# A reordered step list for chunked attention and a phase MLP: the first k pieces on ScalarE's queue, one tile in column halves

## The chip, the cores and the metric

The kernel runs on one core of a Trainium2 chip. The metric is the device time of one execution in microseconds (us). Engines are named as in the profile: PE is TensorE (PEld its weight loads), DVE is VectorE, ACT is ScalarE, POOL is GpSimd, SP is SyncE; a q behind a name (SPq, ACTq, POOLq) is the engine's sequencer that issues DMAs.

## The reference

q, k and v have the shape (8, 8, 576, 64): batch, heads, tokens, head size. Attention runs inside chunks of 64 tokens; its output, with the heads side by side, is the input x of a second block of width 512. All arrays are float32, and the computation cut to its core is:

```python
scores = 0.125 * np.matmul(q_c, k_c.transpose(0, 1, 2, 4, 3))   # per chunk of 64 tokens
attn = softmax(scores)
x = np.matmul(attn, v_c)                                        # (8, 576, 512) after reshaping
theta = x @ w_theta                                             # 512 x 512
zr, zi = x * np.cos(theta), x * np.sin(theta)
y = einsum('ts,bsd->btd', w_tok_r, zr) + einsum('ts,bsd->btd', w_tok_i, zi)   # 576 x 576 each
u = x + y
out = u + np.maximum(u @ w_ch, 0.0)                             # 512 x 512
```

## The kernel before, in words

**Tiles and groups.** Batches are handled in four pairs, p = 0 to 3. A batch has 576 tokens, 4 tiles of 128 and half a tile of 64. So a pair has nine tiles of 128 tokens: tiles 0 to 3 of its first batch, 4 to 7 of its second, and tile 8, which holds the last 64 tokens of both. Attention runs by groups: A (tiles 0 and 1), B (2 and 3), C (4 and 5), D (6 and 7) and M (tile 8). A step that works on a group is named by pair and group, "0A"; one that works on a tile by pair and tile, "31" is tile 1 of pair 3.

**The order.** Nothing is scheduled by a loop: ORDER is a list of some 560 steps, written out, and the kernel runs through it and emits each step's instructions. Every engine works through its own instructions in this order, and waits on semaphores for what others have to deliver. So ORDER decides, for each engine and each DMA queue, what stands behind what. A step has a kind, what it works on, and a number for the PSUM bank or the SBUF slot that it takes: "S.0B.6" are the scores of group B of pair 0 into bank 6.

**The kinds, by stage.**

- qk and v load a group's q and k, and v (two DMAs for q and k of a full group and four for M; three for v of a full group and two for M), with a cast to float16 on the way, from POOL's queue (L173, L178, L226). Group 0A alone is loaded in float32 by halves of its heads, qk0 and qk1, from SP's queue (L192), and cast by ACT and DVE (cy0, cy1; L210).
- T (or Tq and Tk apart; T0 and T1 for the halves of 0A) turns q and k on DVE by 32 x 32 blocks (L279). S are the scores on PE (L317), E their exponentials on ACT (L347, L359). V0 and V1 multiply with v on PE, four heads each (L381), N0 and N1 divide by the sums on DVE (L396, L398). The result is x.
- X turns x on PE (L413) and xa or xv copies it out of PSUM on ACT or DVE (L433, L431); xd does both in one transposing DMA from SP's queue (L425).
- H is theta on PE (L441; H0 and H1 for one tile each), G cosine and sine on ACT (L463, L464), Z the products zr and zi on DVE.
- lw loads a block of 128 rows of both token weights, lp theta's weights, lc the channel weights, all from POOL's queue (L236, L239, L242). TW turns a token block on PE (L257); twa and twv copy it out on ACT or DVE (L269, L267).
- Y is the token mixing of a tile on PE: nine products with the turned token weights (L521), for pair 0 in three parts, Ya, Yb and Ym. A adds x to it on DVE (L543); x then holds u.
- U turns u on PE (L548) and ua or uv copies it out; ud does both in a transposing DMA from SP's queue (L556). W is the channel product on PE, four products of 512 columns (L566). R is relu plus u on DVE (L571). st, sa and sg store the tile from SP's, ACT's or POOL's queue.
- dm issues matmuls on zeros that nobody reads.

Tile 37 has its channel product, its relu and its store in two column halves (W0, W1, R0, R1, sa0, sa1). The first steps of ORDER are, in words: both halves of 0A's q and k; both casts; T0.0A; then the loads of 0M, 0B, v of 0M, v of 0A, the second token block (lw.01), v of 0B, and theta's weights.

## Time and profile before

| what | value |
|---|---|
| median of 3 runs | 196.32 us (196.22 to 197.8) |
| profiled execution, its own time | 197.53 us |
| span of the profiled execution | 195.5 us |
| granted TensorE clock | 1.00 |
| busy PE / PEld / DVE / ACT / POOL | 176.8 / 91.2 / 136.4 / 84.6 / 89.4 us |
| DMA, moved | 31.99 MB, mean 164 GB/s |

The span runs from the first to the last event of the profiled execution; the profile's times count from its start, and 2.0 us of the execution's own time lie outside it. Busy times are sums over the span. Matmuls are pipelined, so a row of a matmul shows a duration of 380 ns where the next one starts 216 ns later; what a step of several matmuls takes is read from the chain of work, which merges a run of them. An entry in brackets behind a row is the idle time of that row's engine just ahead of it, and what ended it.

### The profile page before, as it was taken

How to read it: one execution, taken by the hardware profiler on the slowest of the kernel's cores; microseconds unless marked ns; L12 is line 12 of the kernel's file. 1: busy time of each engine (PE TensorE's matmuls, PEld its weight loads, DVE VectorE, ACT ScalarE, POOL GpSimd, SP SyncE). 2: the span in 40 equal slices, each digit the busy share in tenths (PEclk: the TensorE clock that was granted, in tenths of full speed). 3: DMA queues.
4: the chain of work that ended last, by engine and by line, in shares of the span. 5: the costliest groups of instructions: out<-in, count | busy, mean ns of one | idle time of the engine just before them, and what ended most of it. 6: DMA issues, size and time to landing. Idle time of an engine off the chain costs nothing.

```text
span 195.5 us, 5940 instructions
## 1 busy us (share of the span) xinstructions
PE 176.8 (90%) x2572; PEld 91.2 (47%) x2572; DVE 136.4 (70%) x245; ACT 84.6 (43%) x107; POOL 89.4 (46%) x128
## 2 busy tenths in 40 slices
PE   1159699969999899999999999999999999999975
PEld 0138355535554554645564434554443444454432
DVE  0446778777788796956986999598718845764742
ACT  4135099625955578497026295620096301200010
POOL 8999479895696479559997000000000100000310
DMA  5999999999999999999999968254668906989876
GB/s 161 179 174 174 189 170 167 121 164 172 127 107 170 169 110 167 179 166 160 125 146 171 125 126 213 46 207 121 134 80 191 269 17 121 235 221 280 286 190 215
DMA packets 103849, 31.99 MB, mean 164 GB/s; under 512 B 95248, under 2 KB 99728, under 8 KB 103824
## 3 DMA queue, kind: packets, MB, share of 16 engines
q0 software_dynamic: 76160, 17.59, 96.1%
q1 hardware_dynamic: 24912, 9.31, 21.5%
q10 hardware_dynamic: 2752, 4.72, 7.5%
q8 instruction: 20, 0.33, 0.7%
q14 instruction: 5, 0.04, 0.1%
HBM read 33.06 MB, written 9.44 MB: 217 GB/s over the span
## 4 chain that ended last, share of the span: by engine, by line
PE 77%; DMA 8%; POOL 4%; DVE 3%; SPq 2%; issue 2%; ACT 2%; POOLq 0%
PE psum L521 35%; PE psum L566 15%; PE psum L441 11%; PE psum L317 5%; PE psum L381 4%; DMA mid<-x 3%; PE psum L413 3%; DMA v<-in_v_dram 3%; DMA uT<-x 2%; SPq L556 2%; PE psum L257 1%; PE psum L548 1%; POOL v L226 1%; DVE x L398 1%; POOL big L173 1%
## 5 line engine op out<-in xcount | busy, mean ns | idle before, releaser
L521 PE MATMUL psum<-zr,wT 128*128 128x512 f16 (+1 forms) x180 | 62.2, 382 | 1.5 <-issue 1.5
L521 PE MATMUL psum<-zi,wT 128*128 128x512 f16 (+1 forms) x180 | 59.2, 380 | 0.0
L521 PEld LDWEIGHTS <-wT 128*128 128x128 f16 (+1 forms) x360 | 30.4, 100 | 35.3 <-issue 2.6
L226 POOL DMA_DIRECT2D v<-in_v_dram x56 | 41.9, 786 | 10.3 <-DMA big<-in_k_dram 5.0
L614 POOL DMA_DIRECT2D out_dram<-mid x6 | 3.3, 551 | 76.3 <-ACT big L463 45.9
L566 PE MATMUL psum<-wch,uT 128*128 128x512 f16 (+1 forms) x148 | 35.1, 374 | 1.0 <-DMA uT<-x 1.0
L441 PE MATMUL psum<-wtheta,mid 128*128 128x512 f16 x144 | 34.6, 388 | 0.8 <-DMA mid<-x 0.5
L543 DVE TENSOR_TENSOR x<-psum,x 128x512 f16<-128x512 f32 x36 | 24.1, 682 | 10.5 <-PE psum L521 10.5
L347 ACT ACTIVATE mid<-psum 128x1024 f16<-128x1024 f32 (+1 forms) x19 | 17.5, 932 | 31.5 <-PE psum L317 27.8
L571 DVE SCALAR_TENSOR_TENSOR mid<-psum,x 128x512 f32<-128x512 f32 (+1 forms) x37 | 24.3, 669 | 7.8 <-PE psum L566 6.4
L463 ACT ACTIVATE big<-psum,pihalf 128x1024 f16<-128x1024 f32 x14 | 15.6, 1113 | 29.3 <-PE psum L441 29.2
L398 DVE TENSOR_TENSOR x<-psum,recip 128x512 f16<-128x512 f32 (+1 forms) x40 | 25.5, 638 | 1.4
L279 DVE STREAM_TRANSPOSE big<-big 128x1024 f32<-128x1024 f32 (+3 forms) x25 | 24.5, 1007 | 0.3 <-DMA big<-in_k_dram 0.2
L441 PEld LDWEIGHTS <-mid 128*128 128x128 f16 x144 | 13.9, 100 | 17.8 <-DMA mid<-x 1.5
L566 PEld LDWEIGHTS <-uT 128*128 128x128 f16 x148 | 13.4, 98 | 15.9 <-DMA uT<-x 1.5
L317 PE MATMUL psum<-big 32*64 32x64 f16 x1152 | 14.8, 199 | 6.2 <-DVE big L279 6.2
L317 PEld LDWEIGHTS <-big 32*64 32x64 f16 x1152 | 12.8, 112 | 11.8 <-DVE big L279 8.1
L396 DVE RECIPROCAL recip<-psum 128x8 f32<-128x8 f32 (+1 forms) x40 | 7.8, 194 | 12.2 <-PE psum L381 12.2
L490 DVE TENSOR_TENSOR zr<-x,big 128x1024 f16<-128x1024 f16 x14 | 9.6, 686 | 9.0 <-ACT big L463 8.8
L151 ACT ACT_TABLE_LOAD x12 | 15.4, 1283 | 0.9 <-PEq L672 0.7
L560 ACT COPY uT<-psum 128x512 f16<-128x512 f16 x8 | 4.6, 590 | 24.0 <-PE psum L548 24.0
L178 POOL DMA_DIRECT2D big<-in_q_dram x15 | 13.8, 917 | 2.0 <-DMA big<-in_k_dram 1.0
(45 smaller groups left out, 150.2 us busy)
## 6 DMA issues: line engine op xcount, KB each, us to landing
out_dram<-mid ACTq DMA_DIRECT2D x16, 256.0 KB, 2.9
big<-in_q_dram POOLq DMA_DIRECT2D x15, 256.0 KB, 6.7
big<-in_k_dram POOLq DMA_DIRECT2D x15, 256.0 KB, 7.3
v<-in_v_dram POOLq DMA_DIRECT2D x40, 64.0 KB, 5.2
out_dram<-mid SPq DMA_DIRECT2D x9, 256.0 KB, 3.0
v<-in_v_dram POOLq DMA_DIRECT2D x16, 128.0 KB, 5.7
out_dram<-mid POOLq DMA_DIRECT2D x6, 256.0 KB, 3.2
out_dram<-mid SPq DMA_DIRECT2D x6, 128.0 KB, 2.8
```

The lines of the kernel that those rows point to most:

```text
L151: nc.scalar.activation(out=first, in_=pihalf, func=func)
L226: nc.gpsimd.dma_start(v16[rows, slot + t, :, 0:D], v[b, :, t0 : t0 + m, :].rearrange("h s d -> s h d"),)
L279: nc.vector.transpose(out.bitcast(FP32).rearrange("p (x l s) -> p x s l", l=32, s=2), in_.bitcast(FP32).rearrange("p (x s d) -> p x s d", ...
L317: nc.tensor.matmul(ps[half[r ^ cc], r, h], t[quarter[c], 1, h, :, e], t[quarter[c], 0, h, :, e], start=(e == 0), stop=(e == 1), tile_posit ...
L347: nc.scalar.activation(out=eT[:, 0:n].rearrange("p r h i -> p (r h i)"), in_=st.pop(("ps_s", p, g)).rearrange("p r h i -> p (r h i)"), fun ...
L398: nc.vector.tensor_tensor(out=x.rearrange("p r (h d) -> p r h d", h=HH), in0=ps[:, :, :, 0:D], in1=recip[:, 0:n].broadcast_to((P, n, HH, D ...
L441: nc.tensor.matmul(ps, xT[:, a, :], wtheta16[:, a, :], start=(a == 0), stop=(a == NDB - 1))
L463: nc.scalar.activation(out=cos, in_=ps, func=AF.Sin, bias=pihalf, scale=1.0)
L521: nc.tensor.matmul(ps[half[b]] if j == MID else ps, w, z, start=(kt == 0), stop=(kt == 2 * KT),)
L543: nc.vector.tensor_tensor(out=x, in0=st.pop(("ps_y", p, j)), in1=x, op=ALU.add)
L566: nc.tensor.matmul(ps, uT[:, a, :], wch16[:, a, cols], start=(a == 0), stop=(a == NDB - 1))
L571: nc.vector.scalar_tensor_tensor(out=out, in0=ps, scalar=0.0, in1=x, op0=ALU.max, op1=ALU.add)
```

## The change

ORDER is written anew from end to end, and three things are done in another way.

- The halves of 0A's k are issued by ACT's queue; those of q stay on SP's. The first half's casts are the other way round (cx0: q on DVE, k on ACT), and T0.0A comes ahead of the second half's casts.
- Behind M's q and k, POOL's queue now has v of 0A, q and k of 0B, v of 0B, theta's weights, v of 0M, and only then the token weights. Group D of pair 0 comes ahead of group C, from its loads to its theta.
- Tile 31 is worked on in column halves from the mixing on: Y0 and Y1 (nine products of 256 columns each), A0 and A1, U0 and U1 (two blocks each), uv0 and uv1 (copies on DVE), Wp (both halves of the channel product with the first two blocks), W0 and W1 (the other two), R0 and R1, st0 and st1. Tile 37 goes back to whole steps, and is the last one.

The numbers of turned and copied tiles by engine change little: X by PE 13 before and after, ud 26 before and 25 now, xa 5 and 8, xv 8 and 5, ua 8 and 6, uv 2 and 4 (and two halves), twa 3 and 1, twv 2 and 4. Of the 35 whole stores SP, ACT and POOL issued 12, 17 and 6 before (and ACT the two halves); now it is 8, 16 and 11 (and SP the two halves). dm goes from ten matmuls to nine.

What POOL issues first, before (big is the array of slots for q, k and the token weights; v_72 is v):

```order
L173 DMA big<-in_q_dram 32x8x128 x2
L173 DMA big<-in_k_dram 32x8x128 x2
L178 DMA big<-in_q_dram 128x8x128
L178 DMA big<-in_k_dram 128x8x128
L226 DMA v_72<-in_v_dram 64x8x64 x2
L226 DMA v_72<-in_v_dram 128x8x64
L226 DMA v_72<-in_v_dram 64x8x64 x2
L236 DMA big<-in_moe_w_tok_r_dram 128x576
L236 DMA big<-in_moe_w_tok_i_dram 128x576
L226 DMA v_72<-in_v_dram 128x8x64
L226 DMA v_72<-in_v_dram 64x8x64 x2
L239 DMA wtheta_69<-in_moe_w_theta_dram 128x4x512
```

and in the change:

```order
L174 DMA big<-in_q_dram 32x8x128 x2
L174 DMA big<-in_k_dram 32x8x128 x2
L227 DMA v_72<-in_v_dram 128x8x64
L227 DMA v_72<-in_v_dram 64x8x64 x2
L179 DMA big<-in_q_dram 128x8x128
L179 DMA big<-in_k_dram 128x8x128
L227 DMA v_72<-in_v_dram 128x8x64
L227 DMA v_72<-in_v_dram 64x8x64 x2
L240 DMA wtheta_69<-in_moe_w_theta_dram 128x4x512
L227 DMA v_72<-in_v_dram 64x8x64 x2
L179 DMA big<-in_q_dram 128x8x128
L179 DMA big<-in_k_dram 128x8x128
```

The three issues of v of 0A have moved ahead of q and k of 0B, theta's weights have moved from behind a token block to ahead of v of 0M, and the rows of the token weights are no longer among the first twelve; q and k of 0D stand there.

What DVE runs first, before (the casts of 0A's k, the turning, then the divisions of 0A):

```order
L146 MEMSET pihalf 128x1
L210 CAST big<-big 128x512 x2
L279 STREAM_TRANSPOSE big<-big 128x8x2x32
L279 STREAM_TRANSPOSE big<-big 64x8x2x32 x2
L279 STREAM_TRANSPOSE big<-big 128x8x2x32 x3
L396 RECIPROCAL recip<-psum 128x8
L398 TENSOR_TENSOR x<-psum,recip 128x2x256
L396 RECIPROCAL recip<-psum 128x8
L398 TENSOR_TENSOR x<-psum,recip 128x2x256
L431 COPY mid<-psum 128x1024
```

and in the change:

```order
L147 MEMSET pihalf 128x1
L211 CAST big<-big 128x512
L280 STREAM_TRANSPOSE big<-big 128x8x2x32
L280 STREAM_TRANSPOSE big<-big 64x8x2x32
L211 CAST big<-big 128x512
L280 STREAM_TRANSPOSE big<-big 128x8x2x32 x2
L397 RECIPROCAL recip<-psum 128x8
L399 TENSOR_TENSOR x<-psum,recip 128x2x256
L280 STREAM_TRANSPOSE big<-big 128x8x2x32
L280 STREAM_TRANSPOSE big<-big 64x8x2x32
L397 RECIPROCAL recip<-psum 128x8
L399 TENSOR_TENSOR x<-psum,recip 128x2x256
```

T0.0A and Tq.0M (64 rows) stand ahead of the second cast now; Tq.0B stands ahead of the first division of 0A, and Tk.0B and Tk.0M ahead of the second.

The end of SP's queue, before (stores and the transposes of ud):

```order
L614 DMA out_dram<-mid 128x512 x2
L556 DMA_TRANSPOSE uT<-x 128x4x128 x5
L614 DMA out_dram<-mid 128x512
L556 DMA_TRANSPOSE uT<-x 128x4x128
L614 DMA out_dram<-mid 128x512 x2
L556 DMA_TRANSPOSE uT<-x 128x4x128 x2
L614 DMA out_dram<-mid 128x512
L611 DMA out_dram<-mid 64x512 x2
L614 DMA out_dram<-mid 128x512
```

and in the change:

```order
L665 DMA out_dram<-mid 128x512 x2
L556 DMA_TRANSPOSE uT<-x 128x4x128 x8
L665 DMA out_dram<-mid 128x512
L556 DMA_TRANSPOSE uT<-x 128x4x128
L665 DMA out_dram<-mid 128x512
L672 DMA out_dram<-mid 128x256 x2
```

One store (st.25) is left between the last nine transposes, where three stood between the last eight; the last transpose is ud.37, and the last two stores are the halves of tile 31.

The code, and the first and last lines of ORDER, in the diff:

```diff
-qk0.0A.0 init.00 pre.00 qk1.0A.1 cy0.0A.2 cy1.0A T0.0A.0 on.00 qk.0M.3 qk.0B.4 v.0M dm.1.0
-S0.0A.2 E0.0A.0 Tq.0M.1 Tk.0M v.0A dm.1.0 T1.0A lw.01.3 v.0B S.0M.1 Tq.0B.5 Tk.0B lp.00 S1.0A.2
-E1.0A V1.0A.4 E.0M.1 V0.0A.0 V0.0M.2 lw.02.4 qk.0C.0 N1.0A S.0B.6 N0.0A E.0B.2 V1.0M.4 X.0A.5
-xv.0A.1 N1.0M TW.01.6 V1.0B.0 N1.0B V0.0B.3 N0.0B X.0B.5 twv.01 H0.0A.6 H1.0A.7 xv.0B.2 H1.0B.5
-lw.03.5 H0.0B.3 G0.0A.0 N0.0M X.0M.6 Z0.0A lw.00.1 G1.0A.1 qk.1M.3 qk.0D.2 G1.0B.0 TW.02.1 v.0C
-Tq.0C.6 Tk.0C xa.0M.2 H.0M.5 Z1.0A G0.0B.3 Z0.0B Z1.0B G.0M.1 TW.03.6 v.1M Z.0M twa.03 Ya.01.3
...
-R.36.2 R.30.6 sg.36 R.24.12 sg.25 Y.31.1 ud.32.6 sa0.37 st.17 A.27 st.30 ud.38.3 sa.22 W.38.2
-R.35.2 W.32.5 A.31 R.38.6 U.31.1 sa1.37 R.32.11 sg.33 ud.27.0 W.27.2 st.24 st.38 ua.31.5 W.31.1
-R.27.9 sa.27 dm.8.5 R.31.12 sg.35 sa.31 st.32
+qk0.0A.0 init.00 on.00 qk1.0A.1 pre.00 qk.0M.2 cx0.0A.3 T0.0A.4 v.0A Tq.0M.0 cy1.0A dm.1.0
+S0.0A.2 E0.0A.0 T1.0A S1.0A.0 qk.0B.5 v.0B lp.00 E1.0A V1.0A.2 V0.0A.0 v.0M Tq.0B.1 N1.0A Tk.0B
+Tk.0M S.0B.4 E.0B.1 V0.0B.2 qk.0D.4 lw.03.5 S.0M.4 E.0M.0 N0.0A N0.0B lw.01.1 V1.0B.5 N1.0B
+X.0A.0 xa.0A.1 v.0D X.0B.4 V0.0M.0 H1.0A.5 xv.0B.2 lw.02.0 V1.0M.4 N1.0M H0.0A.6 G1.0A.3 H1.0B.4
+G0.0A.0 N0.0M Tq.0D.2 Tk.0D G1.0B.1 H0.0B.0 G0.0B.2 X.0M.6 xv.0M.4 qk.0C.4 TW.03.2 twv.03
+qk.1M.5 Z1.0A H.0M.4 S.0D.2 G.0M.5 Z0.0A TW.01.0 v.0C lw.00.1 Z0.0B Ya.03.6 twv.01 Ya.01.4
+TW.02.0 Z1.0B v.1M Z.0M qk.1A.0 E.0D.3 twa.02 V1.0D.2 Yb.03 Ym.03 qk.1B.2 V0.0D.0 Ya.02.5
...
+W.21.4 R.21.8 ud.25.1 ud.30.5 R.20.10 sg.24 ud.38.6 W.38.7 R.38.0 R.33.5 Y.36.0 Y.37.7 sg.21
+U0.31.3 A.36 sg.20 W.25.0 A.37 R.25.10 sg.33 uv0.31.1 Y1.31.7 ud.35.4 A1.31 W.30.0 R.30.5
+ud.36.3 W.36.7 U1.31.3 sg.38 sa.17 sa.22 ud.34.6 sg.30 W.35.0 st.25 R.36.2 sg.36 ud.37.0
+Wp.31.7.2 uv1.31 W0.31 W1.31 W.34.3 R.35.10 W.37.0 R0.31.0 R1.31 R.34.5 sa.34 st.35 dm.8.2
+R.37.2 st1.31 st0.31 sa.37
...
-            for w, ap in enumerate((q, k)):
-                nc.sync.dma_start(
+            for w, (ap, queue) in enumerate(((q, nc.sync), (k, nc.scalar))):
+                queue.dma_start(
...
+    def mix_half(f):
+        def products(p, j, b):
+            st["ps_y", p, j, f] = banks(b)[:, 0 : DM // 2]
+            y_mms(p, j, KTS[""], st["ps_y", p, j, f], columns[f])
+
+        return products
...
+    def w_part(p, j, b0, b1):
+        for c, b in enumerate((b0, b1)):
+            st["ps_w", p, j, c] = banks(b)[:, 0 : DM // 2]
+            w_mms(p, j, c, blocks[0])
+
+    def w_mms(p, j, c, a_blocks):
+        for a in a_blocks:
+            nc.tensor.matmul(
+                st["ps_w", p, j, c], st["uT", p, j][:, a, :], wch16[:, a, columns[c]],
+                start=(a == 0), stop=(a == NDB - 1),
+            )
```

More of the change, by code (lines that the diff above doesn't have):

```diff
@@ L521, in y_mms @@
                 nc.tensor.matmul(
-                    ps[half[b]] if j == MID else ps, w, z,
+                    ps[half[b]] if j == MID else ps, w, z[:, cols],
                     start=(kt == 0), stop=(kt == 2 * KT),
@@ L562, in u_copy, with channel_mms @@
         return copy
[L564 removed]
+    def channel_mms(ps, uT):
         for a in range(NDB):
             nc.tensor.matmul(
[L567 removed]
+                ps, uT[:, a, :], wch16[:, a, :], start=(a == 0), stop=(a == NDB - 1)
             )
```

110 lines of the change are left out of this document (65 added, 45 removed).

## The prediction

> **What bounds the kernel now.** I read the windows first, cut at the places where TensorE starts a new stage. Columns: window and length, then busy time (and instructions) of PE, PEld, DVE, ACT and POOL, the granted clock, the DMA share and GB/s.
>
> ```profile
> 0.00:9.11 9.11, 0.61 (x2) 0.11 (x3) 1.79 (x5) 2.72 (x4) 8.50 (x18) 1.00 0.98 169
> 9.11:16.88 7.77, 5.31 (x209) 4.14 (x209) 4.72 (x9) 2.08 (x4) 7.39 (x11) 1.00 1.98 169
> 16.88:22.09 5.21, 3.62 (x58) 3.18 (x59) 3.57 (x8) 2.11 (x3) 3.08 (x6) 1.00 1.35 190
> 22.09:29.51 7.42, 7.13 (x47) 3.57 (x45) 4.87 (x12) 5.41 (x10) 5.15 (x8) 1.00 1.47 176
> ...
> 41.23:109.48 68.25, 66.22 (x1164) 35.42 (x1165) 54.28 (x98) 38.49 (x48) 50.92 (x68) 1.00 1.82 152
> 109.48:183.14 73.66, 73.12 (x761) 34.10 (x760) 52.78 (x91) 24.40 (x27) 2.21 (x5) 1.00 0.67 160
> 183.14:191.36 8.22, 7.21 (x37) 3.11 (x36) 4.22 (x7) 0.59 (x1) 1.08 (x3) 1.00 0.82 245
> ```
>
> From 22.09 to 191.36 PE is idle for only 3.9 us (0.29, 0, 2.03, 0.54 and 1.01): there the matrix work itself sets the time. Before 22.09 it is idle for 12.5 us (8.50, 2.46, 1.59). So a reordering can gain at the start, or lose anywhere. What ended PE's idle times later on is in the waits of PE (us, times, longest):
>
> ```profile
> PE psum L413 <- DVE x L398: 1.6, 1, 1.6
> PE psum L521 <- issue: 1.5, 1, 1.5
> PE psum L566 <- DMA uT<-x: 1.0, 1, 1.0
> ```
>
> A division on VectorE is late once, and a transpose by DMA near the end. The "issue" of 1.53 waits for nothing that the profile shows; with one more of 0.50 it makes the 2.03 of the fifth window. The timeline of the first 30 us has the two larger waits, for the turned q and k and for v, in brackets, and the steps behind them:
>
> ```profile
> 4.46 0.43 DVE L210 CAST big<-big 128x512 f16<-128x512 f32 x1 [3.59 <-DMA big<-in_k_dram]
> 5.02 0.90 POOL L178 DMA_DIRECT2D big<-in_q_dram  x1
> 5.91 0.90 POOL L178 DMA_DIRECT2D big<-in_k_dram  x1
> 6.78 3.65 POOL L226 DMA_DIRECT2D v<-in_v_dram  x5
> 7.80 0.63 DVE L210 CAST big<-big 128x512 f16<-128x512 f32 x1 [2.91 <-DMA big<-in_k_dram]
> 8.36 3.06 DVE L279 STREAM_TRANSPOSE big<-big 128x512 f32<-128x512 f32 x5
> 9.11 0.64 PE L317 MATMUL psum<-big 32*64 32x64 f16 x32 [6.24 <-DVE big L279]
> ...
> 11.65 0.71 DVE L279 STREAM_TRANSPOSE big<-big 128x512 f32<-128x512 f32 x1 [0.23 <-DMA big<-in_k_dram]
> ...
> 13.90 0.50 PE L381 MATMUL psum<-v,mid 64*64 64x65 f16 x3 [2.13 <-DMA v<-in_v_dram]
> 14.15 0.79 POOL L239 DMA_DIRECT2D wtheta<-in_moe_w_theta_dram  x1
> ...
> 16.48 1.02 ACT L347 ACTIVATE mid<-psum 128x1024 f16<-128x1024 f32 x1 [3.56 <-PE psum L317]
> ...
> 22.09 4.68 PE L441 MATMUL psum<-wtheta,mid 128*128 128x512 f16 x16
> ...
> 29.51 0.39 PE L521 MATMUL psum<-zr,wT 128*128 128x512 f16 x1
> ```
>
> At 8.36 T0.0A follows both casts, though its own half had landed by 4.46. PE's first scores come at 9.11, its first v product at 13.90, its first theta product at 22.09, its first mixing at 29.51. The chain of work that ended last gives v's landing and the prices of whole steps:
>
> ```profile
> 9.68 4.89 DMA v<-in_v_dram
> ...
> 28.95 0.62 PE psum L257 x10
> ...
> 32.35 0.64 PE psum L317 x64
> ...
> 55.40 0.25 PE psum L381 x16
> ...
> 175.41 0.88 PE psum L566 x8
> ...
> 183.14 4.49 DMA uT<-x
> ...
> 189.80 1.73 PE psum L566 x8
> ```
>
> So TW costs 0.62, a full S 0.64, half a V pair 0.25, four matmuls of 512 columns 1.73 / 2 = 0.86, eight of 256 columns 0.88.
>
> **The start, step by step.** (1) The halves. k leaves on ScalarE's queue, and T0.0A no longer stands behind the second half's cast: with k landed at 4.46 and 0.63 for a cast, as the second took, T0.0A starts near 5.1 and S0.0A near 5.8, 3.3 us earlier. That alone buys nothing, for PE then waits for T1.0A, which VectorE reaches only after Tq.0M (M's q, issued as before) and the second cast. I put T1.0A at 9.7, S1.0A near 10.2 and E1.0A at 10.9. The queue itself is costed at zero: what hides it is (2).
>
> (2) v of group A. Before, the third of its DMAs left at 9.68 and landed 4.89 later, at 14.57. Now the three follow M's four, from 5.02, at 3.65 / 5 = 0.73 apiece, so the last leaves at 6.5 and lands at 11.4. V1.0A moves from 13.90 to 11.4.
>
> (3) The price of that is group B's q and k, pushed back by three v issues, 2.2 us. k was issued at 5.91 and its turn began at 11.65, 5.74 later; now 8.1 + 5.74 = 13.85. This is what counts next: Tk.0B to 14.5, S.0B (0.64, and up to 1.07 as it ran in this stretch) to 15.4, E.0B 1.02 to 16.5, V0.0B, S.0M and V1.0B to 17.3, then N0.0B and N1.0B on VectorE. These are rows of VectorE by form:
>
> ```profile
> L398 DVE TENSOR_TENSOR x<-psum,recip 128x512 f16<-128x512 f32 x32 | 22.1, 691 | 1.1
> ...
> L396 DVE RECIPROCAL recip<-psum 128x8 f32<-128x8 f32 x32 | 6.4, 200 | 11.8 <-PE psum L381 11.8
> L279 DVE STREAM_TRANSPOSE big<-big 128x512 f32<-128x512 f32 x8 | 5.2, 678 | 0.2 <-DMA big<-in_k_dram 0.2
> ...
> L503 DVE TENSOR_TENSOR zr<-x,mid 128x512 f16<-128x512 f16 x4 | 1.7, 413 | 2.1 <-ACT mid L463 2.1
> ...
> L267 DVE COPY wT<-psum 128x1152 f16<-128x1152 f16 x2 | 1.5, 752 | 0.4 <-PE psum L257 0.4
> ```
>
> Two divisions of 0.89 from 16.9 end at 18.7, X.0B ends near 19.2, and H1.0A starts at 19.3 against 22.09: 2.8 us earlier. Its two inputs are there: theta's weights leave after v.0B, at 8.98 + 2.2 = 11.2 where it was 14.15, and xa.0A ends near 19.
>
> (4) From H1.0A to the first mixing. PE's own work is four H (3.44), V1.0M (0.13), X.0M (0.23), TW.03, H.0M, S.0D and TW.01: 6.5 us, to 25.8. VectorE is the longer one: two N of M, half a division each (1.2 with the short reciprocals), q and k of D (1.36), M's copy (0.4, as for one tile), twv.03 (0.75) and two Z of a tile (1.66) from 20.7, with a wait for X.0M, end at 26.6. So Ya.03 starts at 26.6 against 29.51, 2.9 earlier, with equal work behind it (S.0D for TW.02).
>
> (5) Behind it VectorE stays without a pause to about 35 (Z0.0B, twv.01, Z1.0B, Z.0M, N and T of D, C and the next M), and Ym.03 waits for Z.0M at 30.8. I take 0.4 off: **2.5 us of lead**. Bounds: 0.5 if every load here lands 2 us later than its median, 3.4 if the whole gain of v reaches the end and Tk.0B is not late.
>
> **The token weights.** They now leave behind v and theta. lw.03 leaves near 15.3 and TW.03 is wanted near 23.4. The DMA issues, with the median us to landing last, say:
>
> ```profile
> big<-in_moe_w_tok_r_dram POOLq DMA_DIRECT2D x4, 144.0 KB, 7.3
> ...
> uT<-x SPq DMA_TRANSPOSE x26, 3.2
> ```
>
> 16.0 + 7.3 = 23.3: in time with 0.1 to spare, so zero here; if they take as long as the slowest v (11.1, below), 3.7.
>
> **Tile 31 in halves.** Its mixing becomes 18 matmuls of 256 columns, its channel product 8; tile 37 goes back from 8 halves to 4 full ones. Eight halves took 0.88 against 0.86 for four full, so the columns cost 0.1 at most; the extra seams between steps cost 0.11 each (a step of four stands at 0.97 in the chain where another precedes it, at 0.86 in a run), some three of them, 0.3. The Trainium skill, TensorE: Matmul & The Clock Gate, section The mechanism, says that a weight load overlaps matmuls in flight only where its row group differs. These loads use all rows, so by that rule each half would pay for its load. The chain's 0.88 for eight halves disagrees: with loads of 98 ns ahead of each it would be 1.6.
>
> **The end.** The last product is now W.37, then R.37 and a 256 KB store, as W.31, R.31 and such a store are now. From the last matmul's end, 189.80 + 1.73 = 191.5, to the span's end stay 4.0 us. Before, W.38 waited 1.01 for a transpose that took 4.49 from issue to landing. Now ud.38 leaves 3.3 us ahead of W.38 and ud.37, behind st.25, about 4.0 ahead of W.37, counted back in PE work. The tiles' own rows:
>
> ```profile
> DMA to landing us min/median/max: 2.4/3.2/5.5
> ...
> DMA to landing us min/median/max: 3.2/5.5/11.1
> ```
>
> (the first for uT, the second for v). By the median nothing waits, by 4.49 1.2 plus 0.5, by the longest 2.2. I take 0.7, 0.3 less than now; with the seams the end is even.
>
> **The "issue" gaps**, 1.53 and 0.50, sit in stretches of many tiny matmuls. The new order keeps as many of these, so I leave the gaps in: zero, bounds -2.0 and +1.5.
>
> **Sum.** Lead 2.5, token weights 0, seams +0.3, transposes -0.3, gaps 0: the span goes from 195.5 to 193.0. The profiled execution took 197.53, 2.0 outside its span and 1.2 over the median; taken off the median, 196.32 - 2.5 = **193.8 us**, 1.3% less.
>
> **Rivals.** *The loads take the lead back.* For it: POOL is busy for 50.9 of the 68 us up to 109.48, the DMA share is above 1.3 in every window shown from 9.11 to there, and steps (3) and the token weights have less than half a microsecond to spare. Against it: the first 22 us leave out v.0M and a token block ahead of theta. With landings 2 us late the lead is 0.5: 195.8. Chance 0.22.
>
> *More than the lead.* If the gaps of 1.53 and 0.50 are an accident of where the program stood, they go: 193.8 - 2.0 = 191.8. For it: only two such gaps stand in the whole trace. Against it: nothing in the profile says what makes them, so nothing says that the new order is spared. Chance 0.15.
>
> *Slower: VectorE blocked in its order.* Tq.0B, Tk.0B and Tk.0M now stand ahead of the divisions of group A, and Tq.0M ahead of the second cast. If k of B takes longer to land than 5.74, all behind it moves one for one, and the lead is gone at 5.74 + 2.5 = 8.2. At the 11.1 of the slowest v the start is 2.9 worse than now: 199.2. Against it: with so little issued ahead, nothing has landed that late before 10 us. Chance 0.10.
>
> *The weight loads show.* If the loads of the halves were not hidden, nine more of 98 ns (nine for the mixing, four for the channel product, four fewer for tile 37) would add 0.9: 194.7. The row:
>
> ```profile
> L566 PEld LDWEIGHTS <-uT 128*128 128x128 f16 x148 | 13.4, 98 | 15.9 <-DMA uT<-x 1.5
> ```
>
> Chance 0.03, since the chain shows them hidden; this is what the Trainium skill's rule, above, would do here. That the halves on ScalarE's queue do not come earlier is no case of its own, since V1.0A waits for v either way.
>
> **How the numbers follow.** The forecast has 0.50, its own range 192.8 to 195.0. The 80% range runs from 191.9 (the second rival) to 196.4 (past the first); the slower rival stays outside. A measurement tells about 1% from no change: 194.36 and 198.28. Below lie two thirds of the forecast (0.34), the second rival (0.15) and a little of the others (0.04): faster 0.53. Above lies most of the slower rival: 0.09. The rest is 0.38.
>
> **What would show it.** Right: the first L317 near 6, V1.0A near 11.4, the first theta product near 19.3, the first L521 near 26.6, and from there the same idle as now. Wrong in (3): Tk.0B later than 14. Wrong for the token weights: PE waits at L257. Wrong at the end: PE waits for uT by more than 1. If the first L521 comes at 26.6 and the end does not move, the lead was lost to waits that PE had not had.

## The result and the profile after

The changed kernel takes **199.13 us** (median of 20 runs, 197.13 to 202.16); the kernel before, on the same chip, 197.35 (20 runs, 194.76 to 199.83). The ratio is 1.0121, 95% interval 1.0093 to 1.0149: 1.2% slower. (The ratio is taken over the runs within 1.5% of the fastest of their kernel, here and below; the two medians alone give 1.009.) The forecast was 193.8, 1.3% faster, with 0.09 on slower. (The three runs that it started from, 196.32, were on the low side of before's twenty.) The profiled execution of the change took 198.12 us with a span of 196.4 (before: 197.53 and 195.5), so the two profiled executions lie 0.6 us apart where the medians lie 1.8 apart. Line numbers shift: the scores are now L318, v L382, X L414, theta L442, TW L258, the dummies L163; the mixing stays L521, W L566, the relu L571.

The windows of TensorE's stages come first, cut at the first scores, the scores of group B, the first theta product and the first mixing, and from 41.23 on at the times of the windows of before (the columns are the same):

```profile
6.21:14.33 8.12, 1.94 (x98) 1.54 (x99) 3.97 (x8) 1.57 (x3) 8.12 (x11) 1.00 1.79 143
14.33:21.07 6.74, 5.36 (x152) 4.48 (x153) 3.54 (x8) 3.03 (x4) 4.00 (x7) 1.00 1.67 184
21.07:29.21 8.14, 8.14 (x120) 4.17 (x117) 5.26 (x14) 6.82 (x13) 5.90 (x10) 1.00 1.48 169
...
41.23:109.48 68.25, 67.06 (x1164) 35.02 (x1163) 55.34 (x97) 41.97 (x53) 51.47 (x68) 1.00 1.82 158
109.48:183.14 73.66, 72.86 (x769) 34.49 (x768) 49.55 (x89) 26.43 (x30) 5.45 (x10) 1.00 0.63 156
183.14:191.09 7.95, 7.36 (x47) 4.07 (x46) 5.45 (x11) 0.00 (x0) 1.64 (x4) 1.00 0.85 232
```

From the first theta product (21.07) to the first mixing (29.21) TensorE has no pause at all: 8.14 of 8.14 us. I had priced that stretch at 6.5 us of its work. The timeline of the start shows where the price fails:

```profile
6.21 0.64 PE L318 MATMUL psum<-big 32*64 32x64 f16 x32 [2.71 <-DVE big L280]
...
10.94 0.66 PE L382 MATMUL psum<-v,mid 64*64 64x65 f16 x32 [0.70 <-ACT mid L360]
...
14.32 1.07 PE L318 MATMUL psum<-big 32*64 32x64 f16 x64 [2.73 <-DVE big L280]
...
16.52 0.72 PE L382 MATMUL psum<-v,mid 64*64 64x65 f16 x16 [1.12 <-ACT mid L348]
17.17 1.06 PE L318 MATMUL psum<-big 32*64 32x64 f16 x32
18.16 0.44 PE L382 MATMUL psum<-v,mid 64*64 64x65 f16 x16
18.53 2.00 PE L414 MATMUL psum<-id,x 128*128 128x128 f16 x16
...
21.07 1.89 PE L442 MATMUL psum<-wtheta,mid 128*128 128x512 f16 x4
...
23.25 2.81 PE L442 MATMUL psum<-wtheta,mid 128*128 128x512 f16 x12
...
26.87 1.04 PE L442 MATMUL psum<-wtheta,mid 128*128 128x512 f16 x4
...
29.21 0.39 PE L521 MATMUL psum<-zr,wT 128*128 128x512 f16 x1
```

The first scores (6.21), the first v product (10.94) and the scores of group B (14.32) are where the forecast had them (near 6, 11.4, 14.5). Behind them the same four theta products take 1.89 us at 21.07 and 1.04 at 26.87: start to start they are (1.89 - 0.61) / 3 = 0.43 us apart at first and (1.04 - 0.39) / 3 = 0.22 later, with 0.61 and 0.39 the rows of a single product of that size, a dummy at 2.9 and the first mixing. TensorE runs at half its rate until about 23.4. The page's row PEclk shows 9 in every slice here, and the windows 1.00, so the products' spacing tells it and the granted clock of the page does not.

The waits of TensorE behind the start, by what ended them (total, times, longest):

```profile
PE psum L382 <- ACT mid L348: 1.1, 1, 1.1
PE psum L318 <- issue: 0.8, 1, 0.8
PE psum L566 <- ACT big L465: 0.8, 1, 0.8
...
PE psum L566 <- DMA uT<-x: 0.6, 1, 0.6
PE psum L442 <- issue: 0.3, 1, 0.3
```

The "issue" waits have moved and are shorter (1.53 and 0.50 became 0.84 and 0.34), the wait for a transpose at the end fell from 1.01 to 0.59, and a wait for ScalarE is new. Last, VectorE at the end:

```profile
190.63 0.69 DVE L571 SCALAR_TENSOR_TENSOR mid<-psum,x 128x512 f32<-128x512 f32 x1 [0.33 <-PE psum L566]
192.31 0.69 DVE L571 SCALAR_TENSOR_TENSOR mid<-psum,x 128x512 f32<-128x512 f32 x1 [0.98 <-DMA out_dram<-mid]
```

The last relu waits 0.98 us for a store to leave its slot. From the start of the last product to the span's end it is 196.4 - 191.1 = 5.3 us, where before it was 195.5 - 191.15 = 4.3. The last product starts at the same time in both profiles, so the 0.9 us between the two spans all lie behind it.

### The profile page after: what moved, and what is told of

Same layout as the page of the kernel before. It is cut to its first block, busy times and chain, and to the rows that moved or that the text cites. A ratio compares the mean times of both kernels' runs of the same rounds, so it can differ in the third digit from the quotient of the medians.

```text
span 196.4 us, 5985 instructions
## 1 busy us (share of the span) xinstructions
PE 177.2 (90%) x2584; PEld 91.6 (47%) x2584; DVE 136.0 (69%) x249; ACT 88.1 (45%) x110; POOL 93.6 (48%) x135
## 5 line engine op out<-in xcount | busy, mean ns | idle before, releaser
L521 PE MATMUL psum<-zr,wT 128*128 128x512 f16 (+2 forms) x185 | 61.8, 375 | 0.2 <-DVE wT L268 0.2
L521 PE MATMUL psum<-zi,wT 128*128 128x512 f16 (+2 forms) x184 | 59.4, 374 | 0.0
L521 PEld LDWEIGHTS <-wT 128*128 128x128 f16 (+1 forms) x369 | 31.2, 100 | 33.6 <-issue 0.8
L665 POOL DMA_DIRECT2D out_dram<-mid x9 | 5.0, 552 | 79.3 <-DVE mid L571 77.1
L566 PE MATMUL psum<-wch,uT 128*128 128x512 f16 x140 | 34.5, 380 | 1.4 <-ACT big L465 0.8
L442 PE MATMUL psum<-wtheta,mid 128*128 128x512 f16 x144 | 34.8, 387 | 0.3 <-issue 0.3
L543 DVE TENSOR_TENSOR x<-psum,x 128x512 f16<-128x512 f32 x35 | 23.2, 679 | 11.0 <-PE psum L521 10.9
L571 DVE SCALAR_TENSOR_TENSOR mid<-psum,x 128x512 f32<-128x512 f32 (+1 forms) x37 | 24.0, 669 | 8.5 <-PE psum L566 6.1
L280 DVE STREAM_TRANSPOSE big<-big 128x1024 f32<-128x1024 f32 (+3 forms) x25 | 25.1, 1017 | 4.7 <-DMA big<-in_q_dram 4.1
L399 DVE TENSOR_TENSOR x<-psum,recip 128x512 f16<-128x512 f32 (+1 forms) x40 | 25.5, 638 | 1.4
L318 PE MATMUL psum<-big 32*64 32x64 f16 x1152 | 15.4, 199 | 9.0 <-DVE big L280 8.2
L442 PEld LDWEIGHTS <-mid 128*128 128x128 f16 x144 | 13.4, 99 | 16.1 <-issue 1.2
L318 PEld LDWEIGHTS <-big 32*64 32x64 f16 x1152 | 13.0, 112 | 16.0 <-DVE big L280 9.0
L566 PEld LDWEIGHTS <-uT 128*128 128x128 f16 x140 | 12.6, 98 | 14.7 <-DMA uT<-x 1.1
L465 ACT ACTIVATE big<-psum 128x1024 f16<-128x1024 f32 x14 | 14.3, 1019 | 0.0
```

Source lines behind the costliest of these rows:

```text
L280: nc.vector.transpose(out.bitcast(FP32).rearrange("p (x l s) -> p x s l", l=32, s=2), in_.bitcast(FP32).rearrange("p (x s d) -> p x s d", ...
L318: nc.tensor.matmul(ps[half[r ^ cc], r, h], t[quarter[c], 1, h, :, e], t[quarter[c], 0, h, :, e], start=(e == 0), stop=(e == 1), tile_posit ...
L399: nc.vector.tensor_tensor(out=x.rearrange("p r (h d) -> p r h d", h=HH), in0=ps[:, :, :, 0:D], in1=recip[:, 0:n].broadcast_to((P, n, HH, D ...
L442: nc.tensor.matmul(ps, xT[:, a, :], wtheta16[:, a, :], start=(a == 0), stop=(a == NDB - 1))
L521: nc.tensor.matmul(ps[half[b]] if j == MID else ps, w, z[:, cols], start=(kt == 0), stop=(kt == 2 * KT),)
L543: nc.vector.tensor_tensor(out=x, in0=st.pop(("ps_y", p, j)), in1=x, op=ALU.add)
```

## The experiments

Each was timed beside the kernel before on one chip; the ratio is to that, with its 95% interval. Kernels that were timed together share their runs of before, whose medians are 197.28 us (kernels 1 to 4), 197.65 (5 to 8), 197.15 (9 to 12) and 197.09 (13 to 16). Step names are those of ORDER. They are numbered: 1 is the change once more, 2 has another slot for the last relu, 3, 5 and 10 have products of zeros in the start, 4 is the kernel before with the loads of the change, 6 the kernel before with zeros, 7 and 9 repair late waits, 8 has tile 31 whole, 11 joins 9 and 10, 12 is the kernel before once more, 13 and 15 change slots round, 14 starts late, and 16 has k on SyncE's queue.

### The change once more, and the last relu's slot

The first repeats the change; the second has one edit:

```diff
-R.37.2 st1.31 st0.31 sa.37
+R.37.12 st1.31 st0.31 sa.37
```

> The changed kernel once more, for a second profile and for the time beside the others. If the profiled execution is typical, the span is 196 to 198 and PE's last product ends near 191.5, with a final division of the end (the last relu) waiting 1 us for a store. If the run-to-run spread comes from PE's 'issue' gaps (instructions that arrive late), these gaps lie at other places, but again at the same count of PE instructions modulo 256.

> The changed kernel with one number changed: the relu of tile 37, the last one, writes into slot 12, which has been free for long, where it took slot 2, out of which tile 36 is still being stored. Theory A (the end is longer because the last relu waits for that store, 0.98 us in the profile): about 1.0 us less than the changed kernel, from the last matmul to the end about 4.0 us where it was 4.9. Rival B (the end is set by the queue of stores whatever the slot): no difference of over 0.3 us.

The repeat took 198.82 us (1.0092, 1.0056 to 1.0128), with its first mixing at 30.51: the start varies by over a microsecond from one execution to the next. In the seven profiles that share the change's start as it is, the first mixing stands between 29.2 and 30.5, in an eighth (k's halves on SyncE's queue, below) at 31.5; in two profiles of before it is 29.51 and 29.62. So of the lead of 2.9 us nothing is left. With the other slot: 198.58 (1.0083, 1.0047 to 1.0119). The relu's wait is gone from its profile, but the stretch from the last product to the end is still 4.7 us (4.9 in the repeat, whose relu waits 0.68), and the time is within the intervals of the repeat. The wait alone was not what the end cost.

### Is it the half rate? Products of zeros in the waits

```diff
-S0.0A.2 E0.0A.0 ... V0.0A.0 v.0M ... S.0B.4 E.0B.1
+S0.0A.2 dm.5.7 E0.0A.0 ... V0.0A.0 dm.6.7 v.0M ... S.0B.4 dm.2.7 E.0B.1
```

> The changed kernel with 13 more matmuls on zeros, into a bank that nobody uses then, in the idle times of PE before 16.5 us. Theory C (the array runs at half rate until it has been busy for a few us, so the step prices of the forecast were half of what the start costs): M's scores take 0.3 to 0.4 us where they took 1.06, the two turnings of x 0.45 each where they took 1.0, the first theta product 0.9 where it took 1.9, and the first token mixing starts at 26.5 to 27.5 instead of 29.2; the end moves by up to 2 us. Rival D (the loads and VectorE's order set the start anyway): the first mixing stays at 28.8 or later.

201.07 us (1.0216, 1.0169 to 1.0262). Its PEclk row and its start:

```profile
PEclk9997599999999999999999999999999999999998
```

```profile
14.68 0.71 PE L318 MATMUL psum<-big 32*64 32x64 f16 x64 [0.57 <-DVE big L280]
15.32 0.61 PE L163 MATMUL psum<-zeros 128*128 128x512 f16 x2
...
17.20 1.06 PE L318 MATMUL psum<-big 32*64 32x64 f16 x32
...
18.56 2.00 PE L414 MATMUL psum<-id,x 128*128 128x128 f16 x16
...
21.10 1.89 PE L442 MATMUL psum<-wtheta,mid 128*128 128x512 f16 x4
```

The array was warm when S.0B ran (0.71 us instead of 1.07), and cold again from 17.2 to 24.0, the dip in the fourth and fifth slices: the full rate lasted 3.4 us, in which TensorE was idle for about 1.4, and the half rate came back for 6.8. So this kernel did not test the theory, since X and theta ran as cold as in the change. Its late waits are longer than the change's (1.85 us at W.12, below). It shows how a warm array is lost. The Trainium skill, "TensorE: Matmul & The Clock Gate", section "What's actually happening", has a window of 3.4 us that runs freely, and a full rate after one busy window. The 3.4 us agree with that window, and 6.8 are two of them; the one busy window does not agree, since two went by before the rate came back, and a window that was a good half busy was enough to lose it. The granted clock of an execution tells of such a dip: by an estimate, 6.8 us at half rate in 196 make 1 - 3.4 / 196 = 0.983, and the two profiled executions that show it, of the third and the thirteenth kernel, have 0.980 and 0.983.

The next kernel had more zeros (7 ahead of the first scores, 6, 1, 10, 6 and 2 in the waits and 2 ahead of X.0B):

> The changed kernel with more matrix products of zeros than the third experiment had, placed so that TensorE has work from 2.9 us on in nearly every wait of the start: 7 before the first scores (in place of 1), 6 behind them, 1 behind S1.0A, 10 behind V0.0A, 6 behind S.0B, 2 behind V0.0B and 2 ahead of X.0B. Nothing else is changed and nothing is left out. Theory C (the rule of the array's half rate: it was cold from V0.0B to 23.4, and that took the lead): the granted clock is 1.0 from before 14 us without a break, the 16 transposes L414 take 1.0 us instead of 2.00 and the first theta L442 0.9 instead of 1.89; the first theta product starts at 19.3 to 20.0 (21.07 in the change) and the first mixing product at 26.6 to 27.5 (29.21). The time then falls by 1.7 to 2.6 us, to 196.3 to 197.3. Theory D (the start is held by VectorE, ScalarE or loads, and the matrix array's rate is covered by them): with the array warm, waits on VectorE or ScalarE grow by as much as the products shrink, first mixing at 28.5 or later, and the time stays at 199.

200.51 us as the median of six; the ratio (1.0105, 1.0034 to 1.0176) goes by the three at a granted clock of 1.00, 198.32 to 199.60. Its profiled execution ran at a granted clock of 0.75 from about 10 us to its end (235 us, mean 0.761), so its steps can't be read. The sixth kernel, the kernel before with zeros in its waits, is left out: its last four products of zeros go into bank 7 while that still holds the end of the turned token block TW.01, so it computes something else. The third try, the tenth kernel, takes the zeros away that made useful work late (from the change):

```diff
-dm.1.0 S0.0A.2 ... S1.0A.0 ... V0.0A.0 ... S.0B.4
+dm.7.0 S0.0A.2 dm.6.7 ... S1.0A.0 dm.1.7 ... V0.0A.0 dm.9.7 ... S.0B.4 dm.3.7
```

> The changed kernel with fewer products of zeros than the fifth experiment had, so that they end before the work behind them is ready: 7 ahead of the first scores, 6 behind S0.0A, 1 behind S1.0A, 9 behind V0.0A, 3 behind S.0B, and none after that. Theory C (the half rate took the lead): full rate from 14 us on; V0.0B at 16.5, the 16 transposes L414 take about 1.0 us, the first theta starts at 19.1 to 19.8 and the first mixing at 26.6 to 27.5 (29.21 in the change); the time falls by 1.7 to 2.6 us, to 196.5 to 197.3. Theory D (VectorE, ScalarE or a load holds the start behind V0.0B): the array waits between them as much as its products shrink, first mixing at 28.5 or later.

200.31 us (1.0139, 1.0083 to 1.0195). The start, in the profile:

```profile
15.14 0.71 PE L318 MATMUL psum<-big 32*64 32x64 f16 x64 [1.90 <-DVE big L280]
...
17.58 0.69 PE L318 MATMUL psum<-big 32*64 32x64 f16 x32
...
18.46 0.84 PE L414 MATMUL psum<-id,x 128*128 128x128 f16 x10
19.64 0.51 PE L414 MATMUL psum<-id,x 128*128 128x128 f16 x6 [0.34 <-DVE x L399]
...
20.51 1.04 PE L442 MATMUL psum<-wtheta,mid 128*128 128x512 f16 x4
...
27.64 0.39 PE L521 MATMUL psum<-zr,wT 128*128 128x512 f16 x1
```

Now the rate holds: the transposes take 1.35 us instead of 2.00, the four theta products 1.04 instead of 1.89, and the first mixing is at 27.64, 1.6 us earlier than in the change though S.0B came 0.8 later. Theory C is right on the start. It is wrong on the time: the 1.6 us do not arrive at the end. Counted at the same product, this kernel is 0.85 us ahead of the change at 100 us and level with it at 112; at W.12 it waits 1.86 us where the change waits 0.80, and from there on it is 1.2 behind.

### The loads alone, in the kernel before

```diff
-qk.0B.4 v.0M dm.1.0 S0.0A.2 E0.0A.0 Tq.0M.1 Tk.0M v.0A ... v.0B ... lp.00
+v.0A qk.0B.4 v.0B lp.00 v.0M dm.1.0 S0.0A.2 E0.0A.0 Tq.0M.1 Tk.0M
```

> The kernel before with the start's loads alone in the order of the change: v of 0A ahead of q and k of 0B, v of 0B and theta's weights ahead of v of 0M and the first token weights. Forecast's theory (v gates the start): PE's first product with v moves from 13.9 to 11.4, the first theta product by 1 to 2 us, and the end by as much: 1 to 2 us less than before. Theory C (the array is cold there, and what v gains is idle time later): the first mixing moves by less than 1 us and the time by less than 0.5 us.

202.71 us (1.0286, 1.0224 to 1.0349). The first v product came at 12.56 instead of 13.90, and then TensorE waited 5.45 us for v of group M, since V0.0M stands ahead of S.0B in the old order. So it is no test of what v's loads gain. Moving loads without the products that wait for them makes the start 4 to 5 us longer (first theta product at 26.22 instead of 22.09, first mixing at 34.66 instead of 29.51), and that length arrives at the end almost one for one. That is what it shows.

### Parts of the change undone: k's queue, tile 31

```diff
-for w, (ap, queue) in enumerate(((q, nc.sync), (k, nc.scalar))):
+for w, (ap, queue) in enumerate(((q, nc.sync), (k, nc.sync))):
```

> The changed kernel with the first pieces of k on SyncE's queue again, behind those of q: part one of the change undone. My forecast gave this part nothing. The halves of k then arrive later by as much as a queue's issue takes, 0.5 to 1.2 us; the first scores start at 6.5 to 7.3 instead of 6.21, and the first V and everything from S.0B on (which waits for loads of group 0B) stays where it is: time 199.1 as the change. If the part matters, S.0B and the first mixing move by 0.5 us or more, and the time by as much.

199.26 us (1.0128, 1.0074 to 1.0181), the change's own time. The first scores were even a little earlier (6.02), S.0B later (15.60). Nothing that the times can tell.

```diff
-Y0.31.5 ... A0.31 ... U0.31.3 ... uv0.31.1 Y1.31.7 ... A1.31 ... U1.31.3
+Y.31.5 ... A.31 ... U.31.3 ... uv.31.1
-Wp.31.7.2 uv1.31 W0.31 W1.31 W.34.3 R.35.10 W.37.0 R0.31.0 R1.31 ... st1.31 st0.31
+W.31.7 W.34.3 R.35.10 W.37.0 R.31.0 ... st.31
```

> The changed kernel with tile 31 whole again: one group of 9 products of 512 columns at the place of the first half, its sum, four transposes, a copy and four products W at the place of the last halves; one relu and one store. It undoes one part of the change. My forecast's price for the halves was 0.3 us: the time falls by 0.3 or stays (198.5 to 198.9). If the halves are the loss (theory B), the time falls by 1.0 or more. If they serve the end (the last product W, its relu and store in two pieces), the time rises by up to 0.8, with last product to span's end longer than 5.27.

199.82 us (1.0155, 1.0095 to 1.0214): not faster than the change and rather slower. The halves are not the loss; if anything they serve the end.

### The late waits

SyncE's queue and ScalarE at 120 us in the change, and what TensorE waits for:

```profile
119.58 6.79 SPq L556 DMA_TRANSPOSE uT<-x  x5
```

```profile
116.93 1.28 ACT L152 ACT_TABLE_LOAD   x1
...
119.36 1.28 ACT L152 ACT_TABLE_LOAD   x1
...
121.76 1.01 ACT L465 ACTIVATE big<-psum 128x1024 f16<-128x1024 f32 x1
123.42 1.68 ACTq L665 DMA_DIRECT2D out_dram<-mid  x2
125.20 1.11 ACT L464 ACTIVATE big<-psum,pihalf 128x1024 f16<-128x1024 f32 x1 [2.43 <-DMA uT<-x]
```

```profile
127.28 1.02 PE L566 MATMUL psum<-wch,uT 128*128 128x512 f16 x4 [0.80 <-ACT big L465]
```

W.12 takes the bank that G.2D reads on ScalarE. G.2D stands behind the stores of tiles 05 and 06 on ScalarE's queue, and these wait for nothing of their own, as the program's semaphores say (DMAHW0 to 7 are given round to the DMAs of ScalarE's and SyncE's queues alike, so a DMA that gets a number waits for the earlier one that had it):

```
90 L665 DMA out_dram<-mid 128x512 [waits DMAHW5_49,DMAHW0_49,DVE_49]
91 L665 DMA out_dram<-mid 128x512 [waits DMAHW1_49]
92 L665 DMA out_dram<-mid 128x512 [waits DMAHW2_49]
93 L665 DMA out_dram<-mid 128x512 [waits DMAHW3_49]
94 L464 ACTIVATE big<-psum,pihalf 128x1024 [waits DVE_49,PE_49]
```

By the profile the earlier ones are transposes of SyncE's queue, five in 6.79 us. ScalarE is idle for 2.43 us with its work ready. In the repeat the wait was 0.90, in the second and third kernels 1.14 and 1.85. The two table loads, with which ScalarE changes between exponentials and sines, are a rival: the change has 14 of them where before has 12, at 1.28 us each, and the two more stand between 100 and 145 us. No run takes them away, so what they cost is not known.

```diff
-... sa.05 sa.06 G.2D.9 ... R.37.2
+... G.2D.9 sa.05 sa.06 ... R.37.12
```

> The changed kernel with G.2D.9 (trigonometry of group 2D on ScalarE) moved ahead of the two stores sa.05 and sa.06 on ScalarE's queue, and with the last relu's result in slot 12 instead of 2. Theory A (late waits that the new order has and the old one had not: W.12 at 127 waits 0.8 to 1.1 us for G.2D, and R.37 0.98 us for slot 2): both waits go, and the time falls by 0.8 to 1.8 us, to 197.0 to 198.0. If what stands behind W.12 waits elsewhere, the stall turns up again before 140 us and the time stays at 198.6.

199.25 us (1.0088, 1.0045 to 1.0132): no gain. The wait turned up again behind W.12, at 131 us (1.03, behind the relu R.12, which itself waited 2.36 us for the store of 06, now later, to leave its slot), and the profile has 1.66 at 106 for a copy on ScalarE. So the three stores 01, 05 and 06 were taken off ScalarE's queue, and Y.17 was moved ahead to cover the wait at 106:

```diff
-G.2A.4 v.3C R.13.9 V1.2C.4 H.2M.0 Y.17.1 ... sa.01 ... sa.05 sa.06 G.2D.9 ... R.37.2
+G.2A.4 v.3C R.13.9 Y.17.1 V1.2C.4 H.2M.0 ... sg.01 ... sg.05 sg.06 G.2D.9 ... R.37.12
```

> The changed kernel with five edits behind 100 us and none in the start: the products Y.17 moved ahead of V1.2C and H.2M (they then cover the wait for the copy xa.2M, whose slot is held by a store), the stores 01, 05 and 06 moved from ScalarE's queue to GpSimd's (so that G.2D doesn't stand behind them), and the last relu's result in slot 12. Nothing is left out. Theory A (the late waits are what makes the change slower): the waits at 106 (up to 1.7 us), at W.12 (0.8 to 1.1) and of the last relu (1.0) go, and the time falls by 1.5 to 2.5 us against the change, to 196.3 to 197.3, about that of the kernel before. Theory B (it is the start: a lead that is not there, with the late waits of a size that the kernel before has too): each wait turns up elsewhere and the time stays above 198.3.

197.89 us, **1.0049** (1.0021 to 1.0078), against 1.0121 and 1.0092 for the change and its repeat. W.12's wait is gone:

```profile
PE psum L521 <- ACT mid L465: 0.9, 1, 0.9
...
PE psum L566 <- DMA uT<-x: 0.7, 1, 0.7
PE psum L521 <- DVE mid L571: 0.5, 1, 0.5
```

```profile
122.33 1.01 ACT L465 ACTIVATE big<-psum 128x1024 f16<-128x1024 f32 x1
123.25 1.11 ACT L464 ACTIVATE big<-psum,pihalf 128x1024 f16<-128x1024 f32 x1
```

G.2D now follows its neighbour without a pause. Some waits near 106 to 111 remain (0.53 and 0.87).

### The kernel before once more, and both repairs in one

> The kernel before, unchanged, for a second profile of it: how much its own gaps move from one execution to the next. The waits of TensorE for nothing that the profile shows (1.53 and 0.50 us at 41 and 64 us) are put down to TensorE's instructions arriving late in blocks of 256, behind a full DMA: then the gaps stand at the same instructions, 0 to 2 us long, and the sum of idle time behind the first mixing differs by up to 2 us. If they are a fixed wait of the program, both lengths come again within 0.1 us. The first mixing starts at 29.2 to 30.2; time 197.3.

197.60 us, 1.0031 (0.9996 to 1.0066) to its own runs: so much is the difference of two sets of runs of one program, and the ninth kernel's 197.89, timed with it, is not told from it. Its "issue" waits:

```profile
42.67 0.38 PE L521 MATMUL psum<-zr,wT 128*128 128x512 f16 x1 [1.34 <-issue]
...
101.27 0.60 PE L317 MATMUL psum<-big 32*64 32x64 f16 x51 [0.42 <-issue]
...
108.02 0.22 PE L381 MATMUL psum<-v,mid 64*64 64x65 f16 x4 [0.77 <-issue]
```

The first comes again at the same instruction, the one at 64 us does not, and two others do. Counted in TensorE's instructions, these waits stand at numbers 1217, 3265 and 3521, in the first profile at 1217 and 1985, in the change at 3265 and 3521: always a multiple of 256 apart; the repeat of the change has one, at 3521. There are 20 transfers of 16,384 bytes on the instruction queue, one for about 256 of TensorE's 5,144 instructions (2,572 products and as many weight loads), and TensorE resumes 1.4 to 1.6 us after the end of one (in this run 41.27 and 42.67). So we take the waits for instructions that come late.

> The two kernels above in one: the products of zeros in the start and the five late edits. If both theories A and C hold, their gains add up: span 193 to 194.5, time 195 to 196.3, faster than the kernel before (197.3) by 0.5 to 1.2%. If only one holds, the time of that one.

197.65 us, 1.0048 (1.0022 to 1.0073). The first mixing stands at 27.76, 1.7 us ahead of the ninth kernel's 29.46, and the time is the ninth's. The first mixing in the ninth and in the eleventh:

```profile
29.46 0.39 PE L521 MATMUL psum<-zr,wT 128*128 128x512 f16 x1
```

```profile
27.76 0.39 PE L521 MATMUL psum<-zr,wT 128*128 128x512 f16 x1
```

Where most of the lead goes is seen in the eleventh:

```profile
39.64 0.46 PE L258 MATMUL psum<-id,big 128*128 128x128 f16 x4 [1.07 <-issue]
```

At instruction 1217 again: TensorE, being earlier, waits for its instructions where the ninth kernel did not. Counted at the same product, the lead over the ninth kernel is 1.7 us up to 36 us, 1.6 at 38, 0.4 from behind this wait up to 108, and 0.1 from 113 on; the last product starts 0.3 later than the ninth's (191.09 and 190.79).

### What takes the lead? Three more

ScalarE's copy xa.2M, and all behind it, waits for a store of tile 7 to leave its slot: it starts 5.1 to 7.3 us after the store's issue, at 104.9 to 107.4 in seven profiles. The next two test whether that takes the lead; the first of them gives the copy another slot:

```diff
-xa.2M.6 ... R.13.9 ... G.2M.6
+xa.2M.9 ... R.13.6 ... G.2M.9
```

> The eleventh kernel (products of zeros in the start and the five late edits) with the slots of three results changed round: the copy xa.2M and G.2M in slot 9 instead of 6, the relu R.13 in slot 6 instead of 9. Nothing is left out. ScalarE's copy then waits for the theta products of group 2A (which end at 104.5 to 105.5 with the lead) and no longer for the store of tile 7, which landed at 104.9 to 107.4 in seven executions, 5.1 to 7.3 us after its issue, whatever the lead. Theory E (behind that store ScalarE does G.2A and G.2M, whose banks the matrix work needs next, so a lead in the start is taken away at 105 us): the copy comes up to 1 us earlier, the idle time of TensorE from 105 to 111 (1.28 us in the eleventh run's profile) falls below 0.6, and the time falls by 0.5 to 1.2 us, to 196.4 to 197.2. If it is TensorE's own work between 100 and 112 or its fetches, the copy's place changes nothing: 197.6.

> The ninth kernel (the five late edits alone, no products of zeros) with the slots changed round as in the thirteenth. Without the lead the theta products of group 2A end at about 106.6, later than the store of tile 7 lands: the copy xa.2M comes later by up to 1.5 us, G.2A is not earlier, and the time stays or rises by up to 0.6: 197.9 to 198.5.

198.07 us (1.0059, 1.0027 to 1.0092) with the zeros, 198.74 (1.0074, 1.0042 to 1.0106) without: neither is better than the kernel that it was made from. The first one's profiled execution lost the full rate from 16.9 to about 24 us, as the third kernel had, and had its first mixing at 29.33. So the test of the lead failed in part: TensorE's idle time from 105 to 111 us is 1.25 us there and 1.30 in the eleventh. The slots are no gain. The last of the three takes the lead away again:

```diff
-Z0.0B Ya.03.6
+Z0.0B dm.8.6 Ya.03.6
```

> The eleventh kernel with 8 products of zeros (1.73 us at the full rate) ahead of the first mixing products: they take the lead of the start away again, and nothing else is changed. Theory E (the lead is taken at 105 us in any case): the first mixing starts at 29.4 to 29.6 instead of 27.76, and the time stays within 0.5 us of the eleventh's, 197.2 to 198.1. Theory F (the lead holds and pays to the end): the time rises by 1.5 to 1.8, to 199.1 to 199.5.

198.92 us (1.0105, 1.0058 to 1.0152), 0.6% or 1.1 us more than the eleventh, for a first mixing 2.4 us later (30.14; the loads of group B were 0.8 late as well). That lies between the two theories, and the intervals overlap. But seven of its twelve executions had a granted clock of 0.991 or less (198.4 to 201.2 us), where the rate may have been lost as above. The five at 0.998 or more average 197.7 us, the nine such of the eleventh 197.5 and the eleven such of the ninth 197.9. And counted at the same product, the profiled execution is 1.95 us behind the eleventh's at 34 us, 0.7 from 41 to 113, and 0.2 at the last product. So no more than a few tenths of the lead are seen to pay.

## Why the prediction was wrong, point by point

**(1) and (2), the halves and v of group A**: right. The first scores came at 6.21, v's first product at 10.94; k's queue alone is worth nothing, as forecast.

**(3), to the first theta product**: right up to the scores of group B, wrong behind them. The prices of a full S, half a V pair, X and theta were taken from rows late in the trace, where the array runs at its full rate. The rows of before's own start, which I quoted, had the right price: 16 theta products in 4.68 us from 22.09, where 16 at 0.216 make 3.5, and I had noted 1.07 for S.0B "as it ran in this stretch". S.0M, V1.0B and X ran at half rate, and theta started at 21.07 instead of 19.3. **This is the step that failed**: the prices of TensorE's steps from V0.0B on, here and in (4). V0.0B itself started at 16.52, as forecast. From there to the first mixing the forecast has 10.1 us and the change took 12.7, in which TensorE was idle for 0.2. The warm kernel bears it out: it takes 10.6 (17.02 to 27.64), and theta starts at 20.5 although V0.0B came 0.5 later.

**(4), to the first mixing**: forecast 26.6, measured 29.21 in the change's profile and 29.2 to 30.5 in the others. Of the 2.6 us that were missing in that profile, the half rate took 12.7 - 10.6 = 2.1; the remaining 0.5 lies in the other prices, and in the warm profile partly in waits between ScalarE, VectorE and TensorE (0.41 and 0.34). The rival of late loads is not the cause there: Tk.0B began at 13.56, ahead of the 13.85 that I took. In the six other profiles with the same start it began at 13.7 to 14.3, and the first theta product at the full rate stands anywhere between 23.5 and 25.5 us in the seven; both go into the spread of the start. The full rate comes back no earlier than in before (its first theta product at that rate stands at 24.5 and 24.3 us in two profiles), so the earlier start ran more of its work at half rate: the work grew by what the waits had been. The mean granted clock on the page said 1.00 for this stretch, and I believed it.

**(5), that the lead stays to the end**: wrong in its own right. A lead of 1.7 us, made by warming, gave nothing in the ratio (1.0049 and 1.0048, ninth against eleventh), and about 0.4 us in the executions at a granted clock of 0.998 or more. Instructions arriving late at 39.6 us took 1.1 of it, and 0.3 went around 110 us, where TensorE waits for ScalarE. The forecast took equal work behind an equal start for an equal end; but a wait for something that does not come earlier with the lead takes the lead.

**The token weights and tile 31**: right. No wait of the change's TensorE is for a token weight's load (one of 0.22 us is for the copy of a turned block), and undoing the halves does not make the kernel faster. But the 0.1 to spare was little: in the warm kernel, number 10, TensorE waits 0.37 us for a token block at 38.6.

**The end**: the transposes' wait fell by 0.4, as forecast (0.3). But "from the last matmul's end to the span's end stay 4.0" was wrong by about 1 us. I looked at the DMAs of the transposes there and not at the slots: R.37 stands in a slot whose store has not left (0.98). That wait is hardly the cause, though. With the slot changed, the stretch from the start of the last product is 4.5 to 5.4 us in seven profiles, 5.0 on average, against 5.2 in five with the slot as it was and 4.3 in both of before. There the last relu ends 1.1 us behind that start (1.2 in before), and from its end to the span's end it is 3.4 to 4.3 us (3.2 in before). Why it is longer is open.

**The "issue" gaps**: the zero was about right. They shrank by 0.85 us in the profiled pair, and they vary nearly as much between two executions of one kernel (2.03 and 2.53 before, 1.18 and 0.48 in the change). That was luck as much as judgment: nothing in the forecast said what makes them.

**What made it slower** was in no step: the late waits. W.12 waits for ScalarE and the last relu for a store where the old order waits for neither, and TensorE waits 1.1 and 1.7 us for the copy at 106 in the second and seventh kernels, though not in the change's own two profiles. Five edits that move nothing but these bring the kernel from 1.0121 (1.0092 in the repeat) to 1.0049, as near to 1 as the kernel before comes to itself. That the order as it stood there costs 0.4% to 0.7%, about 1 us, is shown; how it splits among the three is not, since the slot alone and the slot with G.2D gave nothing that could be told, and the two more table loads of ScalarE were not tested. My slower rival had VectorE blocked in the start, another place and another mechanism. No version found is faster than the kernel before.

## What to carry to other kernels

Price a step by rows of its own stretch: the spacing of equal products (0.43 or 0.22 us here) tells a cold array where the clock on the page says 1.00. A lead in the start was worth almost nothing here: late instructions took 1.1 of 1.7 us at one place. And every later wait has to be looked at with the new order: which slot a result takes and whose store still holds it, and which stores stand on the queue of an engine that has work to do. A store on an engine's queue can wait for transfers of another queue, and the engine's work waits with it.

## What the runs showed of the hardware

- **Instructions come in blocks of 256 and can be late.** TensorE stood still for 0.3 to 1.5 us at instructions 1217, 1985, 3265 and 3521 (multiples of 256 apart), 1.4 to 1.6 us behind the end of a 16,384-byte transfer of the instruction queue, while the loads kept the DMA engines busy (163 GB/s from 39.1 to 41.3 us in the kernel before). The Trainium skill, "Runtime: NRT & Kernel Launch", section "Instruction fetch mechanics", has the blocks of 256, and calls the cost of crossing one mostly hidden; these traces disagree, by 2.0 to 2.5 us in the kernel before.
- **The half rate is lost and comes back late**: full rate for 3.4 us with TensorE idle for 1.4 of them, then half for 6.8 in the third kernel, and for about as long (16.9 to 24 us) in the thirteenth. One execution of six of the fifth kernel, which keeps the array busy with zeros from 2.9 us on, had a mean granted clock of 0.761; none of the 42 of the four other kernels that do so went that low, so no run shows that the zeros caused it.
- **A store of 256 KB held its slot for 5.1 to 7.3 us from its issue** near 100 us, with the loads still running, against a median of 2.3 to 3.3 us to landing in the last 11 us.
